# Overlapping the early turns, converting all weights by the fifth pair, and splitting tiles on VectorE

## The chip, the cores and the metric

The kernel runs on one core of a Trainium2 chip. The metric is the device time of one execution in microseconds, the median of several runs. A profiled execution gives the trace that is read here; its engines are TensorE (PE, with its weight loads PEld), VectorE (DVE), ScalarE (ACT), GpSimd (POOL) and SyncE (SP), which issues all DMAs of this kernel.

## The reference

Block-causal attention over 8 batches x 8 heads, 576 positions of 64 dimensions, in blocks of 64, followed by an MLP over the 4608 tokens with 512 inputs and 2048 hidden columns:

```python
scores = q @ k.T / 8            # masked: a query sees the blocks up to its own
attn   = softmax(scores)
x      = (attn @ v).transpose(0, 2, 1, 3).reshape(4608, 512)
h      = x @ w_in               # 512 x 2048
g      = h / (1 + exp(-1.702 * h))
out    = g @ w_out              # 2048 x 512, float32
```

q, k and v are float32; w_in and w_out reach the kernel as 64-bit floats.

## The kernel before

**Pairs and steps.** Two heads are a pair; four pairs are a batch, 32 pairs in all. `step(n)` lists what is issued for pair n, in the order of a string (`ORDER`, one for each of three phases: the first batch, pairs 0 to 3; the second, pairs 4 to 7; all later). In the string, digits are score chunks (`score`), V is the AV product of the pair before (`av`), L is `prep` of the next pair (DVE transposes q and k out of `raw` into `qk`) with the load of the one after that, a, b and c are `flip`, and "-" is an empty slot in which MLP work may come. TensorE's instructions keep the order in which they are written. On the other engines the order is made by a scheduler at compile time from dependences and priorities; each engine then executes its list strictly in that order. A priority with a negative offset puts instructions behind those around them.

**Softmax.** Queries are cut into five chunks: chunk 0 has 64 queries, the others 128, and chunk i sees 64 (2i + 1) keys. For each chunk and head: scores on TensorE into a PSUM bank; a custom DVE reduction adds the mask, scales and takes the maximum (`weigh`, L271); exp on ACT with the sum (L278); DVE adds and inverts (L288, L291); POOL scales (`normalise`, L296). Then the weights must be turned for AV. The early pairs (`early`, n < 8) do it by TensorE transposes against the identity (L92, recorded as matmuls) and ACT evictions (`flip`), later pairs by DVE transposes and DMAs (`turn`). For early pairs the chunks' weights lie in one fixed region, `es`, and the turned ones in `pw`. The AV result is copied by ACT (L369, L370) into `xr`, a ring over two batches: even batches write its first half, odd batches the second.

**Weights.** Products of the MLP are made of three float32r matmuls from high and low parts. `weight_piece` makes a piece of 128 x 2 x 256 weights: SP loads the 64-bit words, ACT scales the upper word (L175), DVE shifts and merges in three instructions (L176, L179, L183), ACT rounds the high part (L187) and POOL subtracts for the low one (L78, a helper's line). There are 32 pieces: for each 256 hidden columns two of w_in (`wih`, `wil`) and two of w_out (`woh`, `wol`). Each piece is handled in two halves. Up to the middle of step 4 the halves are loaded into the yet unused second half of `xr` (`roomy`), four half buffers; after that into three tiles `wst` that share buffers with the output tiles `osb`. `WEIGHTS_BY` says how many half pieces are due at which position (two positions a step). All conversions have the priority offset -200.

**MLP.** Tiles of 384 tokens, 12 in all. `split` makes `xh` (ACT, L401) and `xl` (POOL, L78) from `xr`. For each of 16 chunks of hidden columns: 12 hp matmuls, tanh on ACT (L458), a product on DVE (L459), a high part on ACT (L462), a low part on POOL; then nine matmuls of the chunk before into three banks `acc`. At the end of a tile three copies to `osb` (L425) and three stores. `TILES_BY` places tile 0 from position 8.4 to 17, that is over steps 4 to 8, and ten tiles over the steps that remain; the last tile comes after all attention.

Line 89 is the helper of all matmuls, 92 that of the transposes, 78 that of the subtractions.

Of the kernel before, what the change touches and what calls it, by code (L numbers as in the profile page):

```python
# [10 lines left out]
F32 = mybir.dt.float32  # L11
F32R = mybir.dt.float32r
U32 = mybir.dt.uint32
AF = mybir.ActivationFunctionType
ALU = mybir.AluOpType
# [7 lines left out]


ORDER = (
# [3 lines left out]
)  # L29


WEIGHTS_BY = ((0, 0), (9, 30), (15, 64))
TILES_BY = ((8.4, 0), (17, 1), (65, -2))


# [1 line left out]
def attention_moe_kernel(  # L37
# [9 lines left out]
    nc = tc.nc  # L47
    B, H, S, D = q.shape
    DM, DF = w_in.shape
    P = 128  # L50
    BLK = 64
    NDC = DM // P
# [8 lines left out]
    NCH = 5  # L61

    sp = ctx.enter_context(tc.tile_pool(name="sp", bufs=1))
    d2 = ctx.enter_context(tc.tile_pool(name="d2", bufs=2))
    ps = ctx.enter_context(tc.tile_pool(name="ps", bufs=1, space=PSUM))

    def f(ap):
        return ap.bitcast(F32)

    def early(n):  # L70

        return n < 2 * HP

    def phase(n):
        return 0 if n < HP else 1 if n < 2 * HP else 2

    def subtract(eng, out, in0, in1):
        eng.tensor_tensor(out=out, in0=in0, in1=in1, op=ALU.subtract)  # L78
# [4 lines left out]
    def bank():  # L83
        tags = ["w0", "w1", "w2", "w3"] + (["acc0", "acc1", "acc2"] if turns["n"] < HP else [])
        turns["bank"] += 1
        return ps.tile([P, 512], F32, tag=tags[turns["bank"] % len(tags)], name="bank")
# [4 lines left out]
    def tr(**kw):  # L91
        return tc.keep_in_program_order(nc.tensor.transpose(**kw))  # L92


    ident = sp.tile([P, P], F32, name="ident")
# [11 lines left out]
    xr = sp.tile([P, NDC, RING], F32, name="xr")  # L107
    xh = sp.tile([P, NDC, TT], F32R, name="xh")
    xl = sp.tile([P, NDC, TT], F32R, name="xl")
# [12 lines left out]
    tw, pw = [  # L122
        turned[:, x : x + 4 * NS].rearrange("p (b s) h c -> p b s h c", b=4) for x in (0, 4 * NS - 4)
    ]
# [4 lines left out]
    es = []  # L129
    for i in range(NCH):  # L130
        w, o = BLK * (2 * i + 1), 2 * BLK * i * i
        es.append(flat[:, o : o + 2 * w].rearrange("p (h k) -> p h k", h=2))

    def width(i):
        return BLK * (2 * i + 1)
# [5 lines left out]
    WC = 256  # L141
# [5 lines left out]
    for fb in range(DF // WC):  # L147
        c = slice(fb * WC, (fb + 1) * WC)
# [8 lines left out]
                tuple(x.rearrange("p (a c) -> p a c", a=2) for x in (src, woh[:, fc], wol[:, fc]))  # L157
            )

    def weight_piece(j, roomy):  # L160
        src, hi, lo = pieces[j]
        halves = []
        for a in range(2):
            if roomy:
                w = xr[:, 2 * (j % 2) + a : 2 * (j % 2) + a + 1, S : S + 2 * WC].bitcast(U32)
            else:
                w = d2.tile([P, 1, 2 * WC], U32, tag="osb", name="wst", bufs=3)
            d = nc.sync.dma_start(out=w, in_=src[:, a : a + 1])
            if j < 3:
                tc.keep_in_program_order(d)  # L170
            halves.append((w, d2.tile([P, 1, WC], U32, tag="wm", name="wm", bufs=3)))
        halves = [(w.rearrange("p a (c t) -> p a c t", t=2), y) for w, y in halves]

        for a, (w, y) in enumerate(halves):
            nc.scalar.activation(out=f(y), in_=f(w[..., 1]), func=AF.Copy, scale=2.0**-112)  # L175
            nc.vector.tensor_scalar(  # L176
                out=y, in0=y, scalar1=3, scalar2=None, op0=ALU.logical_shift_left
            )
            nc.vector.scalar_tensor_tensor(  # L179
                out=y, in0=w[..., 1], scalar=0x80000000, in1=y,  # L180
                op0=ALU.bitwise_and, op1=ALU.bitwise_or,
            )
            nc.vector.scalar_tensor_tensor(  # L183
                out=y, in0=w[..., 0], scalar=29, in1=y,
                op0=ALU.logical_shift_right, op1=ALU.bitwise_or,
            )
            nc.scalar.copy(out=hi[:, a : a + 1], in_=f(y))  # L187
            subtract(nc.gpsimd, lo[:, a : a + 1], f(y), f(hi[:, a : a + 1]))

    conv = {"n": 0, "roomy": True}  # L190

    def convert(upto):
        while conv["n"] < upto:
            with tc.high_priority(offset=-200):
                weight_piece(conv["n"], conv["roomy"])
            conv["n"] += 1


    raw, qk = {}, {}
# [23 lines left out]

    def prep(n):

        qk[n] = d2.tile([P, 2, S], F32, tag="qk", name="qk", bufs=1)
        for x in range(2):
            nc.vector.transpose(out=qk[n][:, x], in_=raw[n][:, x].rearrange("p c d -> p (c d)"))  # L228
        raw.pop(n)
# [91 lines left out]
    def flip(n, chunks):  # L321

        for i in chunks:
            todo = [(j, hd) for j in range(i) for hd in range(2)]
            for x in range(0, len(todo), 4):
                part = todo[x : x + 4]
                bk = bank()
                for y, (j, hd) in enumerate(part):
                    tr(out=bk[:, y * P : (y + 1) * P], in_=es[i][:, hd, j * P : (j + 1) * P], identity=ident)
                s0 = SLOT[i] + part[0][0]  # L330
                nc.scalar.copy(
                    out=pw[:, :, s0 : s0 + len(part) // 2].rearrange("p b s h c -> p (s h) b c"),
                    in_=bk[:, 0 : len(part) * P].rearrange("p (x b c) -> p x b c", b=4, c=32),
                )

        last = [i for i in range(1, NCH)] if 4 in chunks else [0] if 0 in chunks else []
        a = 2 if last != [0] else 0
        for hd in range(2 if last else 0):
            bk = bank()
            for y, i in enumerate(last):  # L340
                tr(out=bk[0:BLK, y * P : (y + 1) * P], in_=es[i][:, hd, i * P : width(i)], identity=ident)
            src = bk[0:BLK, 0 : len(last) * P].rearrange("p (s b c) -> p s b c", b=4, c=32)
            nc.scalar.copy(
                out=pw[0:BLK, a : a + 2, 10 : 10 + len(last), hd].rearrange("p b s c -> p s b c"),
                in_=src[:, :, a : a + 2],
            )

    def av(n):
# [22 lines left out]
        if n + 1 < NPAIR:  # L371
            load_v(n + 1)

    def step(n):

        turns["n"] = n
        now = n < NPAIR

        def item(x):
            if x == "V":  # L380
                return (lambda: av(n - 1)) if n else None
            if x == "L":
                return (lambda: (prep(n + 1), load(n + 2) if n + 2 < NPAIR else None)) if n + 1 < NPAIR else None
            if x in ("a", "b", "c"):
                return (lambda: flip(n, {"a": [0, 1], "b": [2, 3], "c": [4]}[x])) if now else None
            return (lambda: score(n, [int(y) for y in x])) if now and x != "-" else None

        return [item(x) for x in ORDER[phase(n)].split()]


    done = {"split": 0}
# [1 line left out]
    def split(t):  # L393
        t0, tt = TILES[t]
        a = 0
        while a < tt:
            c0 = (t0 + a) % RING
            w = min(tt - a, RING - c0)
            for dc in range(NDC):
                src = xr[:, dc, c0 : c0 + w]  # L400
                nc.scalar.copy(out=xh[:, dc, a : a + w], in_=src)  # L401
                subtract(nc.gpsimd, xl[:, dc, a : a + w], src, f(xh[:, dc, a : a + w]))
            a += w
        done["split"] = t0 + tt

# [6 lines left out]
    def moe():  # L412
        prev = None

        def second(state):
            g_hi, g_lo, fc, acc, t = state
            for c in range(TILES[t][1] // P):
                for gi, (ga, wb) in enumerate(((g_hi, woh), (g_lo, woh), (g_hi, wol))):
                    mm(
                        out=acc[c], lhsT=ga[:, c * P : (c + 1) * P], rhs=wb[:, fc, :],  # L420
                        start=fc == 0 and gi == 0, stop=fc == NFC - 1 and gi == 2,
                    )
                if fc == NFC - 1:
                    osb = d2.tile([P, DM], F32, tag="osb", name="osb", bufs=3)
                    nc.scalar.copy(out=osb, in_=acc[c])  # L425
                    r = TILES[t][0] + c * P
                    nc.sync.dma_start(out=out[r : r + P, :], in_=osb)
                yield 650
# [78 lines left out]
    for n in range(NPAIR + 1):  # L507
        items = step(n)
        for sl, fn in enumerate(items):
            if fn is not None:  # L510
                fn()
            if ORDER[phase(n)].split()[sl] == "V":
                heads_done = 2 * n
            pos = 2 * (n + (sl + 1) / len(items))
            conv["roomy"] = pos < H + 0.5
            convert(min(len(pieces), np.interp(pos, *zip(*WEIGHTS_BY)) / 2))
            lim = quota(pos)
            advance(heads_done, lambda: state["t"] >= lim)
# [30 lines left out]
```

## Time and profile before

| | |
|---|---|
| time, median of 3 runs | 1194.05 us (1193.56 to 1194.39) |
| time of the profiled execution | 1195.4 us |
| its span in the trace | 1193.6 us |
| PE busy | 1117.3 us, 94% |
| DVE busy | 600.5 us, 50% |
| ACT busy | 514.9 us, 43% |
| POOL busy | 465.3 us, 39% |
| mean granted TensorE clock | 0.96 of full |

The shares are means over stages that differ. Matmuls are pipelined, and their ends are modelled, so a busy TensorE need not be at its peak; a low granted clock stretches its busy time. Idle time of an engine that is not the bottleneck costs nothing. In the rows of waits the columns are engine, tile and line that waited, what it waited for, and the total in us, the times, and the longest. In the rows of a timeline they are start in us, length in us, engine, line, operation and tiles.

### The profile page before, as it was taken

Reading aid. Unit: us, or ns where it says so; the run is one execution under the profiler, and the core shown is the slowest. Engines: PE = TensorE matmul, PEld = TensorE weight load, DVE = VectorE, ACT = ScalarE, POOL = GpSimd, SP = SyncE. Lnnn points to the kernel's source line nnn. Section 1 sums busy time; section 2 is a strip of 40 time slices with the busy share of each in tenths; the row PEclk is TensorE's granted clock in tenths of the full one; section 3 lists DMA queues with packets and bytes.
Section 4 is the critical chain, followed back from the end, with each engine's and each line's share of the span. In section 5 each row is a group of like instructions: output and inputs, shape, how many; then the busy total and the mean of one; then the engine's idle time right before and its main releaser. Section 6 shows DMA issues by size and latency. Waiting matters only on the chain. (4 is left out here: it accounts for less than half of the span.)

```text
span 1193.6 us, 20228 instructions
## 1 busy us (share of the span) xinstructions
PE 1117.3 (94%) x6960; PEld 921.8 (77%) x6960; DVE 600.5 (50%) x1896; ACT 514.9 (43%) x1381; POOL 465.3 (39%) x587
## 2 busy tenths in 40 slices
PE   6787687789999999999999999999999999999998
PEld 4456565567888878888888878888888878899997
DVE  4556868675455555445554555554455555411111
ACT  4664556464343344444343343344353343332322
POOL 4545546463343343343343342343343343232322
PEclk9767898789999999999999999999999999999999
DMA  5333534234333323343343323333343333210000
GB/s 109 72 70 97 136 92 118 82 82 96 81 75 90 75 56 94 76 107 80 70 107 80 74 65 88 72 88 80 81 106 71 80 77 90 53 35 1 28 1 27
DMA packets 223399, 91.27 MB, mean 76 GB/s; under 512 B 198208, under 2 KB 198208, under 8 KB 223296
## 3 DMA queue, kind: packets, MB, share of 16 engines
q1 hardware_dynamic: 223296, 89.97, 32.4%
q8 instruction: 55, 0.90, 0.3%
q14 instruction: 48, 0.39, 0.1%
HBM read 45.09 MB, written 9.44 MB: 46 GB/s over the span
## 5 line engine op out<-in xcount | busy, mean ns | idle before, releaser
L78 POOL TENSOR_TENSOR gl<-g,gh 128x384 fp32r<-128x384 f32 x192 | 194.7, 1014 | 501.5 <-ACT gh L462 397.4
L89 PE MATMUL hp<-xh,wih 128*128 128x384 f32 x768 | 275.4, 359 | 23.8 <-DVE g L459 11.9
L89 PE MATMUL hp<-xh,wil 128*128 128x384 f32 x768 | 263.3, 343 | 3.8 <-POOL wil L78 3.3
L89 PE MATMUL hp<-xl,wih 128*128 128x384 f32 x768 | 262.5, 342 | 2.3 <-POOL xl L78 2.3
L89 PE MATMUL acc<-woh,gh 128*128 128x512 f32 x576 | 230.3, 400 | 0.0
L89 PE MATMUL acc<-woh,gl 128*128 128x512 f32 x576 | 228.6, 397 | 0.5 <-POOL gl L78 0.5
L458 ACT ACTIVATE g<-hp 128x384 f32<-128x384 f32 x192 | 94.3, 491 | 312.4 <-PE hp L89 292.2
L89 PE MATMUL acc<-wol,gh 128*128 128x512 f32 x576 | 228.9, 397 | 0.0
L459 DVE SCALAR_TENSOR_TENSOR g<-g,hp 128x384 f32<-128x384 f32 x192 | 106.0, 552 | 221.2 <-ACT g L458 219.7
L89 PEld LDWEIGHTS hp<-xh,wih 128*128 128x128 f32 x768 | 146.3, 190 | 73.7 <-DVE mx L271 26.2
L278 ACT ACTIVATE e<-e,mx 64x64 f32<-64x64 f32 (+4 forms) x240 | 133.0, 555 | 107.2 <-DVE mx L271 107.2
L271 DVE CUSTOM_DVE_ANT_0 e<-bank,mask 64x64 f32<-64x64 f32 (+4 forms) x240 | 91.8, 416 | 147.8 <-PE bank L89 147.5
L89 PEld LDWEIGHTS hp<-xh,wil 128*128 128x128 f32 x768 | 146.8, 191 | 12.0 <-POOL wil L78 7.5
L462 ACT CAST gh<-g 128x384 fp32r<-128x384 f32 x192 | 98.3, 512 | 125.7 <-DVE g L459 125.4
L296 POOL TENSOR_TENSOR e<-e,sm 64x64 f32<-64x64 f32 (+1 forms) x192 | 112.8, 610 | 95.7 <-DVE sm L291 93.5
L89 PEld LDWEIGHTS hp<-xl,wih 128*128 128x128 f32 x768 | 146.9, 191 | 3.3 <-POOL xl L78 3.3
L89 PE MATMUL bank<-qk 64*128 64x320 f32 (+4 forms) x768 | 130.2, 440 | 17.1 <-DVE qk L228 7.9
L89 PEld LDWEIGHTS acc<-woh,gh 128*128 128x128 f32 x576 | 109.3, 190 | 24.9 <-ACT g L458 4.5
L89 PEld LDWEIGHTS acc<-wol,gh 128*128 128x128 f32 x576 | 108.8, 189 | 23.7
L89 PEld LDWEIGHTS acc<-woh,gl 128*128 128x128 f32 x576 | 109.2, 190 | 18.4 <-POOL gl L78 0.9
L89 PEld LDWEIGHTS bank<-qk 64*128 64x128 f32 (+1 forms) x768 | 65.6, 186 | 59.8 <-issue 26.3
L305 DVE STREAM_TRANSPOSE turned<-e 128x128 f32<-128x128 f32 (+1 forms) x192 | 89.8, 494 | 36.7 <-POOL e L296 36.5
(47 smaller groups left out, 1075.1 us busy)
## 6 DMA issues: line engine op xcount, KB each, us to landing
turned<-turned SPq DMA_DIRECT2D x192, 80.0 KB, 2.1
turned<-turned SPq DMA_DIRECT2D x96, 112.0 KB, 2.2
raw<-in_q_dram SPq DMA_DIRECT2D x128, 72.0 KB, 2.5
raw<-in_k_dram SPq DMA_DIRECT2D x128, 72.0 KB, 2.5
out_dram<-osb SPq DMA_DIRECT2D x36, 256.0 KB, 2.5
turned<-turned SPq DMA_DIRECT2D x96, 88.0 KB, 2.1
vp<-in_v_dram SPq DMA_DIRECT2D x64, 128.0 KB, 2.4
wst<-in_moe_w_out_dram SPq DMA_DIRECT2D x20, 256.0 KB, 2.7
```

The lines of the kernel that those rows point to most:

```text
L78: eng.tensor_tensor(out=out, in0=in0, in1=in1, op=ALU.subtract)
L89: return tc.keep_in_program_order(nc.tensor.matmul(**kw))
L271: nc.vector.tensor_tensor_reduce(out=e[0:m, hd, lo:hi], in0=s[0:m, 0 : hi - lo], in1=mk, op0=ALU.add, op1=ALU.min, scale=-0.125, scalar=3e ...
L278: nc.scalar.activation(out=e[0:m, hd], in_=e[0:m, hd], func=AF.Exp, scale=-1.0, bias=mx[0:m, i, hd : hd + 1], accum_out=sm[0:m, i, hd : hd ...
L296: nc.gpsimd.tensor_tensor(out=x, in0=x, in1=sc.to_broadcast([m, width(i)]), op=ALU.mult)
L305: nc.vector.transpose(out=tw[:, :, SLOT[i] : SLOT[i] + i, hd].rearrange("p b j c -> p j b c"), in_=e[:, hd, 0 : i * P],)
L458: nc.scalar.activation(out=g, in_=hp[:, 0:tt], func=AF.Tanh, scale=1.702)
L459: nc.vector.scalar_tensor_tensor(out=g, in0=g, scalar=1.0, in1=hp[:, 0:tt], op0=ALU.add, op1=ALU.mult)
L462: nc.scalar.copy(out=gh, in_=g)
```

## The change

1. *Turns of early pairs.* In the first two phases chunks 2 and 3 (B) and chunk 4 (C) of pair n are flipped in step n + 1, after the first scores of pair n + 1; only chunks 0 and 1 (a) are flipped in their own step. L comes before a and chunk 4. Odd early pairs keep `qk` in the buffer of tag e0, which only later pairs use, so that two pairs' q and k exist at once. Step 8, the first late one, has an order of its own (`HANDOVER`) with B and C of pair 7 in it. Each flip takes the diagonal blocks of its own chunks along, in one bank.
2. *Weights.* `WEIGHTS_BY` has 26 pieces due by position 8 (end of step 3) and all 32 by 9.5 (three quarters of step 4). A piece is loaded with one DMA and converted whole; its buffers are always the two in the second half of `xr`. `wm` has two buffers (whole) in place of three (halves), and `osb` two in place of three.
3. *Split.* The subtraction for `xl` goes from POOL to DVE, and the split's casts and subtractions get the priority offset 300 that the g chain has.

```diff
 ORDER = (
-    "01 V 23 a 4 L b c",
-    "01 - - V 23 - - a - 4 L - b - - c",
+    "01 B C V 23 L a 4",
+    "01 - B - C - V - 23 - L a - 4 - -",
     "01 - - - 23 - - V - 4 - - L - - -",
 )
+HANDOVER = "B C - 01 V - 23 - - - 4 - - L - -"
-WEIGHTS_BY = ((0, 0), (9, 30), (15, 64))
+WEIGHTS_BY = ((0, 0), (8, 52), (9.5, 64))
...
-    def weight_piece(j, roomy):
+    def weight_piece(j):
         src, hi, lo = pieces[j]
-        halves = []
-        for a in range(2):
-            if roomy:
-                w = xr[:, 2 * (j % 2) + a : 2 * (j % 2) + a + 1, S : S + 2 * WC].bitcast(U32)
-            else:
-                w = d2.tile([P, 1, 2 * WC], U32, tag="osb", name="wst", bufs=3)
-            d = nc.sync.dma_start(out=w, in_=src[:, a : a + 1])
-            if j < 3:
-                tc.keep_in_program_order(d)
-            halves.append((w, d2.tile([P, 1, WC], U32, tag="wm", name="wm", bufs=3)))
+        w = xr[:, 2 * (j % 2) : 2 * (j % 2) + 2, S : S + 2 * WC].bitcast(U32)
+        y = d2.tile([P, 2, WC], U32, tag="wm", name="wm")
+        d = nc.sync.dma_start(out=w, in_=src)
+        if j < 2:
+            tc.keep_in_program_order(d)
...
     def prep(n):
-        qk[n] = d2.tile([P, 2, S], F32, tag="qk", name="qk", bufs=1)
+        tag = "e0" if early(n) and n % 2 else "qk"
+        qk[n] = d2.tile([P, 2, S], F32, tag=tag, name="qk", bufs=1)
...
-        last = [i for i in range(1, NCH)] if 4 in chunks else [0] if 0 in chunks else []
-        a = 2 if last != [0] else 0
-        for hd in range(2 if last else 0):
-            bk = bank()
-            for y, i in enumerate(last):
-                tr(out=bk[0:BLK, y * P : (y + 1) * P], in_=es[i][:, hd, i * P : width(i)], identity=ident)
...
+        bk = bank()
+        todo = [(i, hd) for i in chunks for hd in range(2)]
+        for y, (i, hd) in enumerate(todo):
+            tr(out=bk[0:BLK, y * P : (y + 1) * P], in_=es[i][:, hd, i * P : width(i)], identity=ident)
+        src = bk[0:BLK, 0 : len(todo) * P].rearrange("p (x b c) -> p x b c", b=4, c=32)
+        for part in ([0], [1]) if 0 in chunks else (chunks,):
...
+    def order(n):
+        return (HANDOVER if not early(n) and early(n - 1) else ORDER[phase(n)]).split()
...
-            if x in ("a", "b", "c"):
-                return (lambda: flip(n, {"a": [0, 1], "b": [2, 3], "c": [4]}[x])) if now else None
+            if x in ("a", "B", "C"):
+                m, chunks = {"a": (n, [0, 1]), "B": (n - 1, [2, 3]), "C": (n - 1, [4])}[x]
+                return (lambda: flip(m, chunks)) if m >= 0 else None
...
-            for dc in range(NDC):
-                src = xr[:, dc, c0 : c0 + w]
-                nc.scalar.copy(out=xh[:, dc, a : a + w], in_=src)
-                subtract(nc.gpsimd, xl[:, dc, a : a + w], src, f(xh[:, dc, a : a + w]))
+            with tc.high_priority(offset=300):
+                for dc in range(NDC):
+                    src = xr[:, dc, c0 : c0 + w]
+                    nc.scalar.copy(out=xh[:, dc, a : a + w], in_=src)
+                    subtract(nc.vector, xl[:, dc, a : a + w], src, f(xh[:, dc, a : a + w]))
...
-                    osb = d2.tile([P, DM], F32, tag="osb", name="osb", bufs=3)
+                    osb = d2.tile([P, DM], F32, tag="osb", name="osb")
```

More of the change, by code (lines that the diff above doesn't have):

```diff
@@ L158, in attention_moe_kernel @@
             )
-    def weight_piece(j, roomy):
+    def weight_piece(j):
         src, hi, lo = pieces[j]
-        halves = []
-        for a in range(2):
-            if roomy:
-                w = xr[:, 2 * (j % 2) + a : 2 * (j % 2) + a + 1, S : S + 2 * WC].bitcast(U32)
-            else:
-                w = d2.tile([P, 1, 2 * WC], U32, tag="osb", name="wst", bufs=3)
-            d = nc.sync.dma_start(out=w, in_=src[:, a : a + 1])
-            if j < 3:
-                tc.keep_in_program_order(d)
-            halves.append((w, d2.tile([P, 1, WC], U32, tag="wm", name="wm", bufs=3)))
[L172 to L188, printed above, removed]
@@ L190, in attention_moe_kernel @@
-    conv = {"n": 0, "roomy": True}
+        w = xr[:, 2 * (j % 2) : 2 * (j % 2) + 2, S : S + 2 * WC].bitcast(U32)
[3 more added lines that the diff above has]
+            tc.keep_in_program_order(d)
+        w = w.rearrange("p a (c t) -> p a c t", t=2)
+        nc.scalar.activation(out=f(y), in_=f(w[..., 1]), func=AF.Copy, scale=2.0**-112)
+        nc.vector.tensor_scalar(out=y, in0=y, scalar1=3, scalar2=None, op0=ALU.logical_shift_left)
@@ L192, in convert @@
+        nc.vector.scalar_tensor_tensor(
+            out=y, in0=w[..., 1], scalar=0x80000000, in1=y,
+            op0=ALU.bitwise_and, op1=ALU.bitwise_or,
+        )
+        nc.vector.scalar_tensor_tensor(
+            out=y, in0=w[..., 0], scalar=29, in1=y,
+            op0=ALU.logical_shift_right, op1=ALU.bitwise_or,
+        )
+        nc.scalar.copy(out=hi, in_=f(y))
+        subtract(nc.gpsimd, lo, f(y), f(hi))
+    conv = {"n": 0}
     def convert(upto):
@@ L194, in convert @@
             with tc.high_priority(offset=-200):
-                weight_piece(conv["n"], conv["roomy"])
+                weight_piece(conv["n"])
             conv["n"] += 1
@@ L334, in flip @@
                 )
-        last = [i for i in range(1, NCH)] if 4 in chunks else [0] if 0 in chunks else []
-        a = 2 if last != [0] else 0
-        for hd in range(2 if last else 0):
-            bk = bank()
-            for y, i in enumerate(last):
-                tr(out=bk[0:BLK, y * P : (y + 1) * P], in_=es[i][:, hd, i * P : width(i)], identity=ident)
-            src = bk[0:BLK, 0 : len(last) * P].rearrange("p (s b c) -> p s b c", b=4, c=32)
+        bk = bank()
[4 more added lines that the diff above has]
+        for part in ([0], [1]) if 0 in chunks else (chunks,):
+            i, x, a = part[0], 2 * chunks.index(part[0]), 2 if part[0] else 0
+            s0 = 9 + max(i, 1)
             nc.scalar.copy(
-                out=pw[0:BLK, a : a + 2, 10 : 10 + len(last), hd].rearrange("p b s c -> p s b c"),
-                in_=src[:, :, a : a + 2],
+                out=pw[0:BLK, a : a + 2, s0 : s0 + len(part)].rearrange("p b s h c -> p (s h) b c"),
+                in_=src[:, x : x + 2 * len(part), a : a + 2],
             )
@@ L383, in item @@
                 return (lambda: (prep(n + 1), load(n + 2) if n + 2 < NPAIR else None)) if n + 1 < NPAIR else None
-            if x in ("a", "b", "c"):
-                return (lambda: flip(n, {"a": [0, 1], "b": [2, 3], "c": [4]}[x])) if now else None
+            if x in ("a", "B", "C"):
+                m, chunks = {"a": (n, [0, 1]), "B": (n - 1, [2, 3]), "C": (n - 1, [4])}[x]
+                return (lambda: flip(m, chunks)) if m >= 0 else None
             return (lambda: score(n, [int(y) for y in x])) if now and x != "-" else None
-        return [item(x) for x in ORDER[phase(n)].split()]
+        return [item(x) for x in order(n)]
     done = {"split": 0}
@@ L511, in attention_moe_kernel @@
                 fn()
-            if ORDER[phase(n)].split()[sl] == "V":
+            if order(n)[sl] == "V":
                 heads_done = 2 * n
             pos = 2 * (n + (sl + 1) / len(items))
-            conv["roomy"] = pos < H + 0.5
             convert(min(len(pieces), np.interp(pos, *zip(*WEIGHTS_BY)) / 2))
```

## The prediction

> **What bounds the kernel now.** I read the slices of the page first, then a table by stage, then TensorE's waits in the stages that are not full.
>
> ```profile
> span 1193.6 us, 20228 instructions
> ```
>
> ```profile
> PE   6787687789999999999999999999999999999998
> ...
> PEclk9767898789999999999999999999999999999999
> ```
>
> From the tenth slice (29.84 us each) TensorE is full and at full clock. Before that it is neither, so there is something to win only in the first quarter. Where a stage begins is seen in TensorE's timeline: a pair's first score matmuls (64x64) mark the start of its step.
>
> ```profile
> 85.80 0.87 PE L89 MATMUL bank<-qk 64*64 64x64 f32 x8 [0.46 <-ACT turned L343]
> ```
>
> ```profile
> 131.63 2.99 PE L89 MATMUL bank<-turned,vp 128*64 128x128 f32 x60 [2.40 <-DVE mx L271]
> ```
>
> ```profile
> 254.41 0.85 PE L89 MATMUL bank<-qk 64*64 64x64 f32 x6
> ```
>
> Steps 0 to 3 (the first batch's pairs) end at 86, the early steps 4 to 7, with tile 0 of the MLP, at 254; the AV matmuls of pair 4, in step 5, start at 131.6. The table by stage, for all instructions and then for those of the conversions' tile wm alone:
>
> ```profile
> 8.00:86.00 78.00, 62.20 (x400) 40.88 (x400) 41.95 (x168) 47.97 (x146) 38.31 (x51) 0.78 0.37 83
> 86.00:255.00 169.00, 129.97 (x762) 99.43 (x758) 127.47 (x327) 93.00 (x268) 88.73 (x110) 0.82 0.41 106
> 300.00:1050.00 750.00, 742.23 (x4806) 620.25 (x4804) 386.45 (x1278) 310.42 (x825) 277.73 (x351) 1.00 0.36 80
> ```
>
> ```profile
> 8.00:86.00 78.00, 11.68 (x24) 6.60 (x17) 5.98 (x8) 0.78 0.37 83
> 86.00:255.00 169.00, 91.20 (x165) 42.77 (x110) 42.61 (x54) 0.82 0.41 106
> ```
>
> The columns are stage, length, busy PE, PEld, DVE, ACT, POOL, clock (the second table: DVE, ACT, POOL, clock). A piece costs six DVE instructions now, so 24 of 192 are 4 of 32 pieces: in the first batch hardly anything is converted, and the other 28 pieces fall into steps 4 to 7, where they are 91 of DVE's 127 us. In 169 us TensorE did 129.97 x 0.82 = 106.6 us of full-clock work: 39 us went idle, 23 us to the clock. At full clock a step with tile 0's share is 106.6 / 4 = 26.7 us, against 42 now; one of the first batch is 62.20 x 0.78 / 4 = 12.1 us, against 19.5. TensorE's waits in those two stages:
>
> ```profile
> PE bank L92 <- POOL turned L296: 10.3, 19, 1.2
> PE bank L89 <- DVE qk L228: 7.9, 1, 7.9
> ```
>
> ```profile
> PE hp L89 <- ACT wih L187: 11.9, 5, 6.1
> PE bank L89 <- ACT xr L370: 6.1, 2, 5.9
> PE hp L89 <- DVE g L459: 5.5, 2, 3.2
> PE bank L89 <- DMA vp<-in_v_dram: 3.4, 1, 3.4
> PE hp L89 <- POOL wil L78: 3.3, 5, 1.5
> ```
>
> The first two are of 8 to 86 (7.9 is the start, before the first scores), the others of 86 to 255. In the first batch it is the turns waiting for the softmax's scaling. Afterwards it is the weights (11.9 + 3.3), and a chain of in-order DVE work with conversions in it (g, xr, the v loads stuck behind SP).
>
> **Part by part.** *The turns.* Chunks 2, 3 and 4 of pair n are flipped in step n+1, after its scores 0 and 1, and qk has a second buffer (tag e0). Transposes, matmuls and evictions stay the same in work; banks per pair fall from ten to nine. What goes is most of the 10.3 us; what stays is C, the added wait, behind only 01 and B; behind it on TensorE stand the pair's AV and the next scores 23. Whatever chunk 4's chain (reduce, exp, scale) then lacks, two steps' work covers the rest. As weights come into the same steps, I count no gain here of itself. The handover in step 8 moves flips into a step that is full of MLP work: nothing. prep and load move ahead of a and 4 on DVE and SP; the two qk transposes and eight raw loads are as many as before, and the raw loads' wait on qk (the third row below) should shrink.
>
> *The conversions.* Before, pieces were due linearly up to step 7.5. Now 26 of 32 are due by the end of step 3, and all by 4.75. Their buffers are only the two whole ones in xr's second half, which pair 4's AV result overwrites. So everything must be converted before that copy: the point that takes the place of the wait for wih. What is queued behind that copy on ACT are exps, evictions and tanhs, and TensorE runs out of its four banks. I call its time T. After T there are no conversions, and 2.67 steps with MLP work remain: 2.67 x 26.7 = 71 us, 73 at the 742 / 750 of the full stage and a little for handing over. Now they take 254 - 131.6 = 123.
>
> What T costs, from DVE's work. Durations of the three DVE instructions of a half piece (128x256), minimum, median, maximum, and one of them beside POOL:
>
> ```profile
> L176 DVE TENSOR_SCALAR wm<-wm x64: 265/288/1716, 25.1 to 255.8; 128x256 uint32<-128x256 uint32 x64
> L179 DVE SCALAR_TENSOR_TENSOR wm<-wst,wm x36: 405/424/1373, 145.8 to 256.6; 128x256 uint32<-128x256 uint32 x36
> L183 DVE SCALAR_TENSOR_TENSOR wm<-xr,wm x28: 396/813/1227, 26.1 to 144.9; 128x256 uint32<-128x256 uint32 x28
> ```
>
> ```profile
> 98.64 1.08 DVE L176 TENSOR_SCALAR wm<-wm 128x256 uint32<-128x256 uint32 x1
> ```
>
> ```profile
> 98.40 1.18 POOL L78 TENSOR_TENSOR xl<-xr,xh 128x384 fp32r<-128x384 f32 x1
> ```
>
> ```profile
> L459 DVE SCALAR_TENSOR_TENSOR g<-g,hp 128x384 f32<-128x384 f32 x138 | 76.1, 552 | 85.7 <-ACT g L458 84.3
> ```
>
> Undisturbed, a half costs 0.28 + 0.41 + 0.41 = 1.10 us. The mean is (11.68 + 91.20) / 189 = 0.544 each, 1.63 a half: 0.53 more, 0.18 an instruction. The excess looks like waiting for a POOL instruction to end: the 0.28 us shift took 1.08 and ended at 99.72, just after POOL's subtraction at 99.58. A two-input instruction of 384 columns takes 552 ns; against 0.41 for 256 that is 1.1 ns a column, so 0.69 for 512; the shift, an estimate between 0.28 and 0.56, 0.42. A whole piece is then 0.42 + 0.69 + 0.69 = 1.80 us undisturbed, and with three waits of 0.18, 2.3 us, against 3.25 now. If instead the excess goes with length (x 1.48), it is 2.65. I take 2.3, because the row shows a wait that ends with POOL's instruction rather than a slower stream. The Trainium skill, "SBUF — State Buffer", section "Who interferes with whom", says that DVE with two SBUF inputs (or in a two-port mode) and GpSimd shut each other out for a whole instruction. The row agrees, and by that rule the excess counts waits (T = 165 below) and not length (180). It also speaks against the change: a POOL scaling that meets a whole piece's instruction would wait up to 0.69 instead of 0.41, and with ten scalings a step and half of that difference each, this estimate puts T later by 5.33 x 10 x 0.14 = 7 us.
>
> DVE's work up to T: attention (41.95 - 11.68) / 4 = 7.6 a step, x 5.33 = 40; conversions 32 x 2.3 = 74; four g of tile 0, 4 x 0.55 = 2; its split, 4 x 0.55 = 2. Sum 118 us from 8 on. DVE cannot be full: in 86 to 255, where conversions also bounded the pace, it was 127.47 / 169 = 75% busy. 118 / 0.75 = 157, T = 165. The early steps then end at 165 + 73 = 238 instead of 254: **-16 us**. ACT (47.97 + 93.00 now, over all eight steps) and POOL (38.31 + 88.73) stay below DVE.
>
> The other end of T is the buffers' round trip, from SP's timeline and waits:
>
> ```profile
> 12.00 1.92 SPq L168 DMA_DIRECT2D xr<-in_moe_w_in_dram  x4
> ...
> 87.87 2.38 SPq L168 DMA_DIRECT2D xr<-in_moe_w_out_dram  x2
> ...
> 98.24 3.50 SPq L168 DMA_DIRECT2D xr<-in_moe_w_in_dram  x4
> ...
> 119.72 4.94 SPq L168 DMA_DIRECT2D xr<-in_moe_w_out_dram  x4
> ```
>
> ```profile
> SPq L168 <- DVE wm L183: 101.7, 40, 15.7
> SPq L219 <- PE bank L89: 30.1, 8, 9.5
> SPq L212 <- DVE qk L228: 21.2, 5, 10.5
> ```
>
> Four halves, two pieces, are one round. Two rounds took 10.4 us (87.9 to 98.2) and 21.5 (to 119.7). Whole pieces take 2 x 0.95 us of DVE out of a round: 8.5 at best, 16 rounds, T = 12 + 136 = 148. With 10.4, T = 178. DVE's 165 lies between. Behind a waiting weight load on SP are the raw and v loads (30.1 and 21.2 are what they wait themselves), and for v TensorE waits (3.4 above).
>
> *The split on DVE.* 48 subtractions of 384 columns leave POOL (1.18 in the row) for DVE at about 0.55. In the full stage the wait that they could touch is
>
> ```profile
> PE hp L89 <- POOL xl L78: 1.4, 2, 0.7
> ```
>
> so between -1.4 us and, if the priority puts a cast in front of the next chunk's tanh (a copy of 512 columns takes 0.59, below), +0.6 at each of 11 tile ends; DVE is busy 386 of 750 us there, ACT 310. I take -1, since the full stage's TensorE has next to no waits to lengthen.
>
> *osb in two buffers.* At the end the third copy waits for the first store:
>
> ```profile
> L425 ACT COPY osb<-acc x36: 585/587/599, 271.0 to 1189.9; 128x512 f32<-128x512 f32 x36
> ```
>
> ```profile
> 1189.18 1.69 SPq L427 DMA_DIRECT2D out_dram<-osb  x3
> ```
>
> ```profile
> DMA to landing us min/median/max: 2.0/2.5/3.9
> ```
>
> 1189.2 + 2.5 = 1191.7 against the third copy's start at 1189.9: **+1.8 us**. At the eleven other tile ends ACT stalls as long, with exps and tanhs queued behind it and TensorE waiting for those: between 0 and 11 x 1.8 = 20 us. I take 0: TensorE has attention and the next chunk's matmuls in hand there, and the full stage's row has ACT idle for more than half; if that cover is gone, it is the 20.
>
> Sum: -16 - 1 + 1.8 = -15. The profiled execution took 1195.4 us, 1.8 more than its span, and the median of the runs is 1194.05. So 1194 - 15 = 1179 us.
>
> **Rivals.**
> *Better overlap.* Longer-range turns leave DVE fewer holes: 85% busy, 118 / 0.85 + 8 = 147, which is also the best round trip. End 220, 34 us gained: about 1161. For it: the first batch's waits are short and named. Against: no early stage reaches that share.
> *The gain is lost in the buffers.* Rounds stay at 10.4 us, or a whole piece costs 2.65 (74 becomes 85, T = 180): the early steps end near 252, and with osb the time is about 1193, between 1188 and 1198.
> *Slower: two pieces a step.* The instruction order written for DVE and SP could keep a weight load behind the next raw loads and its conversion behind a step's softmax, as in the round of 21.5. Four such rounds, to 12 + 86 = 98 us, are the first batch and give 8 pieces; the other 24 come with TensorE standing before pair 4's copy, 12 rounds of 10.4, T = 223, end 296: 42 us lost, with osb about 1236. It decides from a mean round of 10.6 us on (T = 181). For it: the buffers are fewer than now, when wst adds three halves. Against: pieces due earlier also load and convert earlier, and 40 waits on L183 show that SP mostly waits for conversions.
> *It doesn't do what it says*: if turns overlap but conversions are not earlier, the weights' waits stay, and the time is 1190 or more; counted with the lost gain.
>
> **How the numbers follow.** Forecast 0.50 (1163 to 1188), better overlap 0.12, gain lost 0.16, slower 0.22. Faster by over 0.2% (2.4 us, about what this measurement tells from no change): 0.50 + 0.12 + 0.10 = 0.72; within: 0.04; slower: 0.02 + 0.22 = 0.24. The range 1155 to 1205 holds the forecast, most of better overlap, the lost gain and the mild end of slower, eight in ten; it leaves out the full stall.
>
> **What would show it.** Right: wm instructions end near 165 and the 64x64 scores of pair 8 begin near 238; DVE wm at about 2.3 us a piece; no wait of hp for wih after T; the clock 1.0 from T on; the last copy to osb 1.8 us late. Wrong: a long wait of TensorE or ACT before the copy to xr (L370) of pair 4 (slower), rounds of the weight loads over 10.6 us, or 300 us onward no longer full.

## The result and the profile after

The changed kernel takes 1282.56 us (median; 1281.02 to 1283.46) against 1194.22 for the kernel before on the same chip: a ratio of 1.0738, 95% interval 1.0719 to 1.0756, 88 us slower. The profiled execution has a span of 1279.2 us.

The page's slices (span, TensorE's busy tenths, granted clock), now 32 us each:

```profile
span 1279.2 us, 19955 instructions
...
PE   5307169999989968999989968999989969999998
...
PEclk9657679999999998999999989999989988999999
```

The early stretch is worse, with a slice of no TensorE work at all, and the full stretch is no longer full: dents come again and again. TensorE's waits over the whole execution:

```profile
PE bank L94 <- ACT xr L367: 51.0, 1, 51.0
PE acc L91 <- ACT osb L427: 45.7, 6, 11.8
PE hp L91 <- ACT xh L403: 37.2, 3, 36.4
PE bank L91 <- DVE qk L224: 17.0, 3, 8.0
```

There are two early waits, 51.0 us once and 37.2 us that are nearly all one wait of 36.4, and six late ones, 45.7 us together. By stage (columns as in the prediction):

```profile
180.00:255.00 75.00, 75.00 (x562) 63.06 (x560) 32.26 (x115) 39.22 (x117) 33.25 (x42) 1.00 0.19 33
400.00:600.00 200.00, 183.72 (x1130) 152.50 (x1128) 93.44 (x318) 73.90 (x201) 59.22 (x79) 0.95 0.34 76
```

After the conversions the early steps run full and at full clock. The first two rows are the starts (64x64 scores) of steps 5 and 8; the third is step 9, which began at 284.10 in the kernel before, so the early part lost 15 us and the rest, some 70, was lost later:

```profile
189.26 0.86 PE L91 MATMUL bank<-qk 64*64 64x64 f32 x8
...
272.96 0.86 PE L91 MATMUL bank<-qk 64*64 64x64 f32 x8
299.38 0.86 PE L91 MATMUL bank<-qk 64*64 64x64 f32 x8
```

**The late stall.** One of the six, first on ACT, then on SP, then on TensorE:

```profile
463.40 0.59 ACT L427 COPY osb<-acc 128x512 f32<-128x512 f32 x1
...
465.42 0.58 ACT L427 COPY osb<-acc 128x512 f32<-128x512 f32 x1
...
480.49 0.58 ACT L427 COPY osb<-acc 128x512 f32<-128x512 f32 x1 [10.47 <-DMA out_dram<-osb]
```

```profile
464.56 10.05 SPq L313 DMA_DIRECT2D turned<-turned  x16
474.65 1.19 SPq L207 DMA_DIRECT2D raw<-in_q_dram  x2
475.89 2.12 SPq L207 DMA_DIRECT2D raw<-in_k_dram  x4
478.11 3.33 SPq L429 DMA_DIRECT2D out_dram<-osb  x3
```

```profile
481.13 0.79 PE L91 MATMUL acc<-woh,gh 128*128 128x512 f32 x1 [11.36 <-ACT osb L427]
```

Two of three copies to osb are made by 466, but their stores come behind sixteen DMAs of turned attention weights and six raw loads in SP's list and are issued at 478, 14 us after the first copy. Issuing what stands in front is most of this: the sixteen take 10.05 us one behind the other. With two buffers the third copy waits for a landing, acc's bank stays taken, and TensorE stands for 11.4 us. Three of the six waits are like this one (11.3 to 11.8 us). In the other three, of 3.75 us each, the stores go out 3 to 4 us after the first copy, and the third copy stands behind exps in ACT's own list.

**The early stall.** ACT's list around the copy that releases TensorE at 97:

```profile
92.73 0.66 ACT L172 ACTIVATE wm<-xr 128x512 f32<-128x512 f32 x1 [2.95 <-DMA xr<-in_moe_w_out_dram]
93.29 0.60 ACT L182 CAST wih<-wm 128x512 fp32r<-128x512 f32 x1
96.33 0.58 ACT L367 COPY xr<-bank 128x512 f32<-128x512 f32 x1 [2.44 <-DVE wm L178]
```

It is the wide copy of pair 1's AV result; its narrow one (L366) had run at 44.16. From 48 us on ACT did nothing but conversions, some twelve pieces, and the copy itself waits for DVE's last step of a conversion. The second wait comes the same way: pair 3's wide copy ran at 167.34, behind conversions again, the split's cast (xh) of its row right after it, and with that TensorE went on:

```profile
168.89 0.69 PE L91 MATMUL hp<-xh,wih 128*128 128x384 f32 x1 [36.39 <-ACT xh L403]
```

The trace has a separate semaphore instruction on ACT in front of just two of the wide copies, these two. In the kernel before the wide copies have none:

```profile
L367 ACTq EVENT_SEMAPHORE  x2: 17/17/17, 96.3 to 166.8; - x2
```

The compiled instruction list (from the program, not from a trace) says the same: of the early pairs' copies only those of pairs 1 and 3 carry a wait for DVE. Pairs 1 to 4, with the place of the instruction in ACT's list:

```
65 L367 COPY xr<-bank 128x512 [waits DVE_49,Activation_49]
83 L367 COPY xr<-bank 128x512 [waits PE_49]
121 L367 COPY xr<-bank 128x512 [waits DVE_49,Activation_49]
154 L367 COPY xr<-bank 128x512 [waits PE_49]
```

Those pairs write columns 64 to 576 of the second and the fourth row of xr, the first half. A whole piece's buffer is columns 576 to 1088 of rows 1 and 2, or 3 and 4, as one operand of two rows. The columns never overlap; the halves of before, one row each, carry no such wait.

### The profile page after: what moved, and what is told of

Read it like the earlier page. It is cut to its first block, busy times and chain, and to the rows that moved or that the text cites. A ratio compares the mean times of both kernels' runs of the same rounds, so it can differ in the third digit from the quotient of the medians.

```text
span 1279.2 us, 19955 instructions
## 1 busy us (share of the span) xinstructions
PE 1100.8 (86%) x6960; PEld 921.4 (72%) x6960; DVE 598.9 (47%) x1848; ACT 505.8 (40%) x1317; POOL 409.7 (32%) x507
## 5 line engine op out<-in xcount | busy, mean ns | idle before, releaser
L91 PE MATMUL hp<-xh,wih 128*128 128x384 f32 x768 | 274.1, 357 | 46.8 <-ACT xh L403 37.2
L91 PE MATMUL acc<-woh,gh 128*128 128x512 f32 x576 | 231.3, 402 | 45.7 <-ACT osb L427 45.7
L91 PE MATMUL bank<-qk 64*128 64x320 f32 (+4 forms) x768 | 123.2, 429 | 17.7 <-DVE qk L224 17.0
```

The lines of the kernel that those rows point to most:

```text
L91: return tc.keep_in_program_order(nc.tensor.matmul(**kw))
```

## The experiments

**e1, three output buffers.** All but the osb and wm buffers is the changed kernel; they share, for room.

```diff
-        y = d2.tile([P, 2, WC], U32, tag="wm", name="wm")
+        y = d2.tile([P, 2, WC], U32, tag="osb", name="wm", bufs=3)
-                    osb = d2.tile([P, DM], F32, tag="osb", name="osb")
+                    osb = d2.tile([P, DM], F32, tag="osb", name="osb", bufs=3)
```

> Changed kernel, but the output tiles have three buffers again (the conversions' tile wm shares them, as both are 128 x 2 KB). Theory S (two output buffers, whose stores wait in SP's queue behind the turned copies, hold up the copies of acc and so TensorE): the 45.7 us in which TensorE waits for the copy to osb go, and the lower clock after each stall with them; 1282.6 becomes about 1230, and all before 280 us stays as it is (step 9 still starts near 299). Rival (the late part is slow from the split on VectorE): the late part stays slow, over 1270.

1211.27 us (1209.96 to 1212.93); ratio to the kernel before 1.0147 (1.0132 to 1.0162). TensorE's waits after 300 us are short again, and step 9 starts at 299.58, as expected:

```profile
PE hp L91 <- DVE xl L80: 3.4, 2, 1.7
PE hp L91 <- DVE g L461: 2.9, 3, 1.0
```

The third buffer is worth 71 us, more than the 53 that I expected, and the split, still on VectorE here, is not what slowed the late part. S holds.

**e2, stores from ScalarE's queue.** Two buffers, as changed:

```diff
-                    nc.sync.dma_start(out=out[r : r + P, :], in_=osb)
+                    nc.scalar.dma_start(out=out[r : r + P, :], in_=osb)
```

> Changed kernel with two output buffers, but the stores are issued from ScalarE's queue, right behind their copies. Theory S (SP's order is the cause): a third copy waits only for a landing of 2.1 us, TensorE waits under 5 us for osb in all, about 1232. Rival (two buffers are too few by themselves, as the prediction's +1.8 us and its bound of 20 had it): 10 to 20 us of such waits stay, about 1250.

1213.83 us (1213.03 to 1215.34), ratio 1.0169 (1.0154 to 1.0184). TensorE has no wait for osb left after 300 us. So two buffers are enough when the store is issued behind its copy; it is SP's order that makes them too few.

**e3, narrow AV copies.**

```diff
-        nc.scalar.copy(out=xr[:, h, c0 + BLK : c0 + S], in_=o)
+        cuts = range(0, 512, 128) if early(n) else (0,)
+        for z in cuts:
+            zz = slice(z, z + 512 // len(cuts))
+            nc.scalar.copy(out=xr[:, h, c0 + BLK + zz.start : c0 + BLK + zz.stop], in_=o[:, zz])
```

> Changed kernel, but the AV result of an early pair is copied to xr in four copies of 128 columns in place of one of 512. In the instruction list the copies of pairs 1 and 3 then no longer wait for conversions (their columns never overlap the weights' buffers; with the one wide copy a wait for them was recorded all the same). Theory D (this wait is what stops TensorE for 51.0 and 36.4 us): both waits go; conversions spread into the steps, T between 148 and 178, step 9 starts 20 to 50 us earlier than 299; 1235 to 1262. Rival R (the two buffers' round trip sets T anyway): the waits move to the copy of pair 4, T stays near 178 and the time within 5 us of 1282.

1257.34 us (1255.88 to 1258.84), ratio 1.0532 (1.0514 to 1.0549), 25 us less. Both early waits are gone, and two others have come; TensorE's longest up to 300 us:

```profile
PE bank L91 <- DVE qk L224: 44.9, 6, 19.7
PE bank L91 <- ACT xr L370: 43.8, 1, 43.8
```

The second is the copy of pair 4, the wait that the prediction had: all but the last piece is converted before it (it ran at 177.66, the last conversion step at 181.3). The conversions still end at 182. D and R are each half right: the wait on pairs 1 and 3 was needless and cost 25 us, and behind it stands a T near 180.

**e4, the turns alone.** On the kernel before: `ORDER`, `HANDOVER`, the second qk buffer and `flip` as changed, the rest as before.

> Kernel before with the new turns alone (orders, handover, second buffer of qk, flips), weights, osb and split as before. Theory: the turns help by themselves, about the 10.3 us that TensorE waited for POOL's scaling in the first batch, 1184, as conversions in the second batch are as before. Rival: the second batch is bound by its conversions and takes the gain back, 1192 to 1196.

1174.23 us (1172.61 to 1175.54), ratio 0.9835 (0.9821 to 0.985). In the first batch TensorE's wait for POOL's scaling fell from 10.3 us to this:

```profile
PE bank L94 <- POOL turned L299: 0.2, 1, 0.2
```

Its wait for wih fell too (11.9 to 8.1 us), while that for qk rose, from 7.9 to 26.9. Step 9 starts at 264.05, 20 us earlier. From 8 us to the start of step 9, before and then here (columns as in the prediction):

```profile
8.00:284.10 276.10, 219.65 (x1338) 162.98 (x1339) 186.97 (x550) 156.02 (x453) 141.17 (x179) 0.83 0.38 95
8.00:264.05 256.05, 206.42 (x1339) 160.08 (x1339) 182.19 (x550) 152.91 (x453) 140.36 (x179) 0.86 0.40 102
```

TensorE's idle time fell by 7 us (56.5 to 49.6); the other 13 are the busy time of as many matmuls, at a mean granted clock of 0.86 in place of 0.83. The rival is out: the second batch did not take the gain back.

**e5, both mends** (e1 and e3 together).

> Changed kernel with both mends: AV copies of early pairs in four parts, three output buffers. If the two causes are separate, their gains add: 71 us (three buffers) and 25 us (four copies) off 1282.6, about 1186. If one of them hid behind the other, less is gained, over 1195.

1189.12 us (1187.54 to 1189.53), ratio 0.995 (0.9937 to 0.9964). 93 us of the expected 96: the two causes are separate, and without them the change is no longer slower than the kernel before, but 0.5% faster.

**e6, raw loads from ScalarE's queue**, on e5.

```diff
-                    nc.sync.dma_start(
+                    nc.scalar.dma_start(
                         out=raw[n][r : r + 32, x],
```

> The same with both mends, and the raw loads of q and k issued from ScalarE's queue in place of SP's. Theory R1 (T, the end of the conversions near 182, comes from loads that stand behind each other in SP's order: the weight loads of the second round wait from 24 to 40 us behind raw loads, and raw loads behind weight loads make TensorE wait 45 us for qk): the second round starts before 32, T falls to 155 to 170, TensorE's wait for qk falls below 25, 1165 to 1178. Rival R2 (T is the round trip of two whole buffers, 9.0 us for two pieces, whoever issues what): T stays between 175 and 185 and the time within 5 us of the kernel with both mends.

1243.33 us (1242.73 to 1243.77), ratio 1.0406 (1.0392 to 1.042). A miss. The second round did start early, at 15.1, but the third only at 49.8; the last step of a conversion came at 190.2 and not at 180.5:

```profile
L178 DVE SCALAR_TENSOR_TENSOR wm<-xr,wm x32: 648/692/1643, 14.4 to 190.2; 128x512 uint32<-128x512 uint32 x32
```

Taking the raw loads off SP does not bring T down. It changed ACT's list as well: the first rounding of a piece (L182) ran at 46.3, behind the first pairs' exps and evictions, where it ran at 24.4 in e5. The kernel is also slower late, where TensorE waits 29.4 us for g and 10.6 for osb; ACT now has 256 more DMAs to issue. R1 is out in the form in which I put it; that R2 is all is not shown by it.

**e7, the split alone**, on the kernel before: `nc.vector` and the priority.

> Kernel before with the split's subtraction on VectorE and with priority, nothing else. By the prediction's working -1 us: 1192 to 1195. Rival (casts in front of the next tanh, VectorE's list held up): up to 7 us slower, 1197 to 1201, with longer waits of TensorE for xl or g after 300.

1194.04 us (1192.77 to 1195.41), ratio 0.9995 (0.9986 to 1.0004): no difference. The waits only change places: after 300 us xl 3.4 and g 2.9, where they were 1.4 and 6.4.

**e8, turns and split**, on the kernel before.

> Kernel before with the new turns and the split on VectorE; weights and osb as before. If the split is worth nothing by itself, 1174 as with the turns alone (1172 to 1176); if it frees POOL for the turns of the second batch, 1168 to 1172.

1173.83 us (1173.4 to 1175.0), ratio 0.9826 (0.9812 to 0.9839), as with the turns alone. This is also 15 us less than e5, from which it differs only in the conversions (half pieces, their due times and buffers) and in the narrow copies that the whole pieces call for.

**e9, conversions without the offset**, on e5.

```diff
-            with tc.high_priority(offset=-200):
+            with tc.high_priority(offset=0):
```

> Changed kernel with both mends, and the conversions traced without the offset of -200, so that they come earlier in the engines' lists. If T (182) is 16 rounds of the two buffers of which the first took 28 us because its conversions and the next loads stand behind a pair's own work, the second round starts before 25 and T falls by about 15, to 160 to 170; the AV copy's wait of 43.6 us falls alike, 1172 to 1182. Rival (attention and conversions only change places): T falls, but TensorE waits longer for qk and softmax in the first batch; 1186 to 1195.

1171.41 us (1169.98 to 1172.34), ratio 0.9802 (0.9784 to 0.9821), a little better than expected. The weight loads of the first rounds in SP's timeline, e5 first, then e9:

```profile
11.80 1.01 SPq L167 DMA_DIRECT2D xr<-in_moe_w_in_dram  x2
...
35.59 1.96 SPq L207 DMA_DIRECT2D raw<-in_q_dram  x4
37.59 2.13 SPq L207 DMA_DIRECT2D raw<-in_k_dram  x4
39.81 1.26 SPq L167 DMA_DIRECT2D xr<-in_moe_w_out_dram  x2
```

```profile
12.18 1.02 SPq L167 DMA_DIRECT2D xr<-in_moe_w_in_dram  x2
18.78 0.87 SPq L207 DMA_DIRECT2D raw<-in_q_dram  x2
22.91 3.79 SPq L167 DMA_DIRECT2D xr<-in_moe_w_out_dram  x2
```

The second round starts at 22.9 in place of 39.8, and the last conversion step at 166.3 in place of 180.5; the wait for pair 4's copy falls from 43.6 to 11.4 us, while that for qk stays (45.6). So the compiled order, not a loading limit, set this part of T. With the loads on another queue (e6) but the conversions still behind, T did not fall.

**e10, two output buffers in the kernel before** (osb and wst, which shares them).

> Kernel before with two buffers for the output tiles (and for wst, which shares them) in place of three. Theory S holds without any other part of the change: after 300 us TensorE waits 30 to 60 us for copies to osb, 1250 to 1275. Rival (it takes the changed order of the handover or the split to bring this wait): under 10 us of such waits, 1194 to 1205.

1259.08 us (1258.57 to 1263.28), ratio 1.0536 (1.0514 to 1.0557). The late stall comes without any other part of the change:

```profile
PE acc L89 <- ACT osb L425: 37.4, 6, 9.4
```

Part of the 64 us is early here, since wst has a buffer less too: step 9 starts at 296.86 and not at 284.10.

**e11, turns, split, half pieces, weights due earlier**, on e8:

```diff
-WEIGHTS_BY = ((0, 0), (9, 30), (15, 64))
+WEIGHTS_BY = ((0, 0), (9, 36), (13.5, 64))
```

> Kernel before with turns and split changed, half pieces and buffers as before, and the weights due somewhat earlier: 18 pieces at position 9, all at 13.5. If the second batch of that kernel still waits for weights (8.1 and 3.2 us with the turns alone), some of it goes: 1166 to 1172. Rival: the loads stand in SP's way and nothing is gained, 1173 to 1178.

1169.01 us (1168.63 to 1169.13), ratio 0.9783 (0.9766 to 0.9799): 5 us from the weights.

**e12, the same without the offset.**

> The fastest kernel so far (turns and split changed, half pieces, weights due at 18 pieces by position 9 and all by 13.5; 1169) with the conversions traced without the offset of -200. If holding conversions back costs here what it cost with whole pieces (18 us there), part of it comes off: 1155 to 1165. Rival: here the three further buffers make the rounds short enough, and conversions in front of a pair's softmax only lengthen TensorE's waits for qk: 1168 to 1180.

1166.12 us (1164.41 to 1166.49), ratio 0.9751 (0.9738 to 0.9765), the fastest of all, 29 us under the kernel before, and between what I expected and the rival. 3 us are left of the 18 that the offset cost with whole pieces.

## Why the prediction was wrong

The runs split the 88 us into steps that add up. From the kernel before, turns and split take 20 off (e8); the conversions as changed, with both mends, add 15 (e8 to e5); the waits of two copies add 22 (e5 to e1); two output buffers add 71 (e1 to the changed kernel). The prediction had 0 and -1, -16, nothing, and +1.8. Part by part:

- *osb in two buffers* is the term that failed most: +1.8 us, with "I take 0" for the other eleven tile ends and 20 as the bound. It measures 71 us (e1). I priced the wait as a copy plus a landing of 2.5 us, with a store that goes out at once. That holds at the end of the kernel, where SP has nothing else: the third copy waited 1.4 us there. In the full stage SP executes its list in order, and the profile of before already showed how late a store can be. One of its tile ends, the first copy on ACT and then SP's timeline:

```profile
444.95 0.59 ACT L425 COPY osb<-acc 128x512 f32<-128x512 f32 x1
```

```profile
442.44 10.91 SPq L317 DMA_DIRECT2D turned<-turned  x16
453.44 2.23 SPq L212 DMA_DIRECT2D raw<-in_q_dram  x4
455.71 2.12 SPq L212 DMA_DIRECT2D raw<-in_k_dram  x4
457.93 1.43 SPq L427 DMA_DIRECT2D out_dram<-osb  x3
```

  The store is issued 13 us after its copy began; with three buffers nothing waits for it. At six of the twelve tile ends of that profile the first store comes 3 to 13 us after the first copy, 50 us together; with two buffers TensorE waited at six tile ends, 45.7 us together. The prediction went by SP's queue up to 260 us only. The cover "TensorE has attention in hand" was none: its list is in order too, and acc was next.
- *The conversions, -16 us.* The term that the forecast rests on did not come. With both mends the conversions as changed cost 15 us against the kernel with turns and split alone (1189.12 and 1173.83), and with their offset gone too they are about even with it (e9, 1171.41; the intervals of the ratios overlap). The early steps ended earlier than 254, as forecast (step 8 began at 248.68 in e5 and 232.13 in e9), but the turns alone bring that to 237.63 (e4), which the prediction counted at nothing.
- *What must be converted before what.* The prediction named one copy, pair 4's, as the point T. The copies of pairs 1 and 3 got the same wait, by operands that do not overlap, and TensorE stood 51.0 and 36.4 us. It cost 22 us (e1 to e5) or 25 (e3). No row of the profile before shows it; the instruction list of the change does. It is shown that the wait goes with the width of the copy (e3). That it takes the two-row operand of a whole piece as well fits e4, e8, e11 and e12, which have half pieces and wide copies and show no such semaphore; it was not run by itself, and why such operands get a wait is open.
- *T = 165.* The sum of DVE's work, 118 us, was about right: in the changed kernel, for DVE up to 184 us,

```profile
8.00:184.00 176.00, 70.46 (x527) 53.46 (x528) 118.23 (x271) 84.85 (x215) 77.29 (x79) 0.68 0.46 123
```

  (120.53 up to 182 with both mends), but the share that it can be busy was taken from a stage (75%), and was 118.23 / 176 = 67%. With both mends T is 181, with the conversions not held back 167 (e9), and DVE 125.65 us busy in the 159 up to then, 79%. So the share came out of the order of the lists. The rival "the gain is lost in the buffers", T between 178 and 180 and about 1193, has the numbers of e5 (181 and 1189), but by luck: the rounds were not 10.4 us each. The first two took 28.0 and 17.5, the other fourteen 8.8 on the mean, and the turns' 20 us are in the 1189.
- *The slower rival* (two pieces a round of 21.5 us, 1236) did not set the time. Rounds ran at 7.3 to 7.7 us while TensorE stood (from 73.65 over 81.28, 88.63 to 96.31). But what it described, weight loads behind raw loads in SP's list, is in the first round (28 us) and in the one that began at 96.31 (22 us).
- *A piece costs 2.3 us of DVE.* It measured 77.09 / 32 = 2.41, undisturbed 0.43 + 0.69 + 0.69. That is nearer to a wait for each instruction (2.3) than to an excess by length (2.65):

```profile
0.00:300.00 300.00, 77.09 (x96) 39.11 (x64) 43.46 (x32) 0.81 0.36 90
```

- *73 us after T, 26.7 a step.* Right, counted from TensorE's going on behind pair 4's copy to step 8: 71.0 us in e5 (from 177.68) and 71.3 in e9 (from 160.82). In the changed kernel steps 5 and 6 took 26.2 each.
- *The turns, counted at nothing by themselves.* Mis-sized: 20 us (e4), 7 of them idle time and 13 busy time, at a higher granted clock.
- *The split, -1 us.* No difference (e7).

The step that failed is thus the pricing of waits: a store was taken to go out at once, and two copies were taken to wait for nothing. The -16 failed beside it, as the turns alone bring the early steps about as far. With both causes out the change is 0.5% faster than before, and that is the turns; the conversions, on which the forecast rests, take most of it back. The 1171 us of e9, close to the forecast of 1179, are no confirmation of it: they come with another order of the conversions and with the turns' 20 us.

## What to carry to other kernels

Before a buffer is taken away, look up on which queue its release is issued and what stands in front of it there at that time: the price is the time that this takes there, waits and issuing together, at each use, and not only the transfer's landing. When an operand is made larger (two rows in place of one), look in the compiled instruction list for waits that were not there before, above all on copies that TensorE's next bank hangs on. And where a change has several parts, time them one by one: here the turns alone were worth 1.65%, and the rest of the change buried them.

## What the runs showed of the hardware

A stall costs more than its length. From the start of step 9 to the end, the changed kernel and then the one with three buffers (e1):

```profile
299.38:1279.20 979.82, 916.34 (x5623) 773.85 (x5622) 426.45 (x1384) 358.50 (x927) 282.36 (x357) 0.97 0.29 66
299.58:1210.00 910.42, 899.48 (x5623) 759.04 (x5622) 428.72 (x1384) 358.58 (x927) 281.71 (x357) 1.00 0.31 71
```

Of the 69.4 us between them the waits for osb are 45.7 and longer waits for g and xl 5.0. Another 16.9 are in the busy time of the same 5623 matmuls, 2.8 for each of the six stalls, at a mean granted clock of 0.97 in place of 1.00. The first matmul after the stall at 481 took 0.79 us, where such a matmul has a mean of 0.40, and the hp matmuls behind it started every 0.32 us up to 486, where they start every 0.17 to 0.18 at full clock. The Trainium skill, "TensorE: Matmul & The Clock Gate", Part 1, says that the clock drops to half after an idle window of about 3.4 us and comes back after about as long a busy one. Half speed for one or two such windows is an estimate, from that figure, of 1.7 to 3.4 us for each stall. The trace agrees: 2.8.
